# A gated mix of windowed attention and a state-space convolution: channel order within a chunk, the transposition of x, and the loading of the parameters

## The chip, the cores and the metric

The kernel runs on one core of a Trainium2 chip. The metric is device time in microseconds: the median of three runs is 471.79 us (470.23 to 472.16). The core has five engines with a queue of instructions each, worked off in order: PE (matrix products, with separate weight loads, PEld), ACT and DVE (elementwise work; both can read the matmul results in PSUM), POOL and SP (here they mainly issue DMAs). ACT, SP and POOL each issue DMAs on a queue of their own.

## The reference

x has 2048 positions and 640 channels. The result is `g * a + (1 - g) * b`, position by position.

```python
g = _sigmoid((x * gate_w).sum(-1, keepdims=True))
# a: 32 heads of 20, each query sees 8 keys at distances 0, 2, ..., 14
qkv = (x @ wqkv).reshape(B, S, 3, H, Dh)
logits = jnp.einsum("bhsd,bhswd->bhsw", q, kg) * Dh ** -0.5
a = einsum("bhsw,bhswd->bhsd", softmax(logits), vg).reshape(B, S, D) @ wo
# b: one kernel of length 2048 per channel out of 192 complex modes, then a causal convolution by FFT
P = jnp.exp((dt * A)[:, :, None] * l[None, None, :])
K = jnp.einsum("dn,dnl,dn->dl", Cc, P, dt * Bc).real
y = irfft(rfft(pad(x)) * rfft(pad(K)))[:L] + x * Dskip
```

A = A_re + i A_im, Bc and Cc likewise, are 640 x 192 each; dt = exp(log_dt) is one number for each channel.

## The kernel before

**Parameters.** `SSMParams.loads` brings the six 640 x 192 tensors into SBUF as 128 partitions x 5 x 192, channel 5p + k in partition p at k: one DMA each, three on SP's queue and three on ACT's, followed on SP by four quarters of x in its natural layout (`xn`, L67) and on POOL by five slices of wqkv (L68). `part` turns them into phases and magnitudes, split into 12 bf16 pieces per mode, in two parts: k = 0 alone (part A, all at once) and k = 1 to 4 (part B, whose steps are spread over the first ticks of what follows). Each piece is written to a DRAM buffer `Sprm` by SP (L372, L374) and comes back, chunk by chunk, as `L` (`load_L`, L476, SP).

**Chunks.** `KGen.chunk` works on 64 channels at a time, ten chunks (c = 0 to 9). For a chunk, PE forms arguments in PSUM (L498), ACT takes their sine (L509, 12 instructions) or exponential (L516, 6), DVE multiplies, and PE sums over the modes (L550). Every such ACT instruction is followed by `drain`, which advances a tick; 18 ticks make a chunk. At a tick `tick_hook` inserts work of other parts into the instruction streams: a step of part B, steps of the projections (`late`), and steps of the attention (`core`, 0.56 steps per tick from tick 25 on).

**Attention.** `window` transposes the first half of x on PE, with the identity, ahead of the chunks: 40 matmuls (L85) into PSUM and five ACT copies (L86) to `xT`. `late` has 70 steps: 15 projections of the first quarter of positions, ten transposes of the second half (L105, L106), 45 projections. A projection is five accumulating matmuls of 128x512 (L140) and an ACT copy (L142); one or two of them make a store on POOL's queue (L144) to q, k or v in DRAM, from where `core` loads them (L182 to L184, POOL). The gate is computed from all of xT at tick 31.

**FFT.** After the chunks, x and the kernels go through a first DFT stage (L651, evacuated by `copy_on`, L691 on ACT and L693 on DVE, in turn), a second (L739, L742), a product, and an inverse: 20 groups of 16 matmuls 64x128 (L768) into PSUM tiles `cp`, each copied to `C` by `copy_on` (ACT or DVE), then the last stage (L782) and the output. `C` holds 160 channels contiguously for each of 128 rows; `chan(c, q)` says at which of the 80 places of a half the channel q of chunk c lies. With 5p + k as above, neighbouring channels of a chunk lie 5 apart.

What `copy_on` writes for group cb, four channels l:

```python
def chan(c, q):
    return 40 * (c % 2) + 5 * q + c // 2
x0 = chan(cb // 2, 4 * (cb % 2))
dst = C.rearrange("p x (c q) -> p x c q", c=2)[:, :, :, x0:x0 + 16:5]
copy_on(nc, cb, dst, cp[:].rearrange("p c l x -> p x c l"))
```

Of the kernel before, what the change touches and what calls it, by code (L numbers as in the profile page):

```python
# [10 lines left out]
ACT = mybir.ActivationFunctionType  # L11
ALU = mybir.AluOpType
AX = mybir.AxisListType
F32 = mybir.dt.float32
BF16 = mybir.dt.bfloat16
# [6 lines left out]
D = 640  # L22
# [5 lines left out]
NKT = 5  # L28
SC = 512
# [18 lines left out]
class Attn:  # L48
# [10 lines left out]
    def loads(self, bufA, xn, cst):  # L59
# [3 lines left out]
        self.xn = xn  # L63
        xr = self.x.rearrange("(i p) d -> p i d", p=128)
        wr = self.wqkv.rearrange("(k p) c -> p k c", p=128)
        self.gw = cst.tile([128, NKT], BF16, name="gw_sb")
        xl = [lambda sc=sc: nc.sync.dma_start(xn[:, 4 * sc:4 * sc + 4], xr[:, 4 * sc:4 * sc + 4]) for sc in range(4)]  # L67
# [3 lines left out]
    def window(self, cst, pa):  # L71

        nc = self.nc
        xn, xT, ident = self.xn, self.xT, self.ident

        def zeros():
            zz = cst.tile([128, 5, HALO], BF16, name="zz")
            nc.vector.memset(zz[:], 0.0)
            nc.gpsimd.dma_start(self.kS[:, :, 0:HALO], zz[:])
            nc.gpsimd.dma_start(self.vS[:, :, 0:HALO], zz[:])  # L80

        def transpose(hf, kt):
            tx = pa.tile([128, 2, 512], F32, name="ar")
            for i in range(8):
                nc.tensor.matmul(tx[:, i // 4, (i % 4) * 128:(i % 4) * 128 + 128], xn[:, 8 * hf + i, kt * 128:(kt + 1) * 128], ident[:], start=True, stop=True)  # L85
            nc.scalar.activation(xT[:, kt, 1024 * hf:1024 * hf + 1024], tx[:].rearrange("p a b -> p (a b)"), ACT.Identity)  # L86
        zeros()
        for kt in range(NKT):
            transpose(0, kt)
# [9 lines left out]

    def transposes(self, sc):  # L100
        nc = self.nc
        for kt in range(NKT):
            tx = self.slot()
            for i in range(4):
                nc.tensor.matmul(tx[:, i * 128:i * 128 + 128], self.xn[:, 4 * sc + i, kt * 128:(kt + 1) * 128], self.ident[:], start=True, stop=True)  # L105
            nc.scalar.activation(self.xT[:, kt, SC * sc:SC * sc + SC], tx, ACT.Identity)  # L106
            yield
# [21 lines left out]
    def proj(self, wk, sc):  # L129
# [3 lines left out]
        for which, dstS, off in ((0, self.qS, 0), (1, self.kS, HALO), (2, self.vS, HALO)):  # L133
            for e in range(5):
# [8 lines left out]
                if e % 2 == n - 1:  # L143
                    nc.gpsimd.dma_start(dstS[:, e + 1 - n:e + 1, off + c0:off + c0 + SC], t[:, 0:n])  # L144
                yield

    def late(self, wk):
        yield from self.proj(wk, 0)
        for sc in range(2, NSC):
            yield from self.transposes(sc)  # L150
        for sc in range(1, NSC):
            yield from self.proj(wk, sc)
# [12 lines left out]
    def load_wo(self):  # L165
        self.nc.gpsimd.dma_start(self.wo_sb[:], self.wo.rearrange("(p e) c -> p e c", e=5))
# [99 lines left out]
def chan(c, q):  # L266

    return 40 * (c % 2) + 5 * q + c // 2
# [39 lines left out]
class SSMParams:  # L308
# [5 lines left out]
    def loads(self, ctx, tc, A_re, A_im, B_re, B_im, C_re, C_im, log_dt, gate_w, ident, gw_sb, pa, xl, wl):  # L314
# [3 lines left out]
        self.t = t = {}  # L318

        def load(eng, nm, ap):  # L320
            t[nm] = pin.tile([128, 5, NST], BF16, name=nm)
            eng.dma_start(t[nm][:], ap.rearrange("(p k) n -> p k n", k=5))
        ldt = pin.tile([128, 5], BF16, name="ldt")
        lg5 = pin.tile([5, 128], BF16, name="lg5")
        nc.sync.dma_start(ldt[:], log_dt.rearrange("(p k) -> p k", k=5))
        load(nc.sync, "cre", C_re); load(nc.scalar, "bre", B_re)
        load(nc.sync, "cim", C_im); load(nc.scalar, "bim", B_im)
        load(nc.sync, "aim", A_im); load(nc.scalar, "are", A_re)
        nc.sync.dma_start(lg5[:], gate_w.rearrange("(k p) -> k p", p=128))
        xl[0](); xl[1]()  # L330
        for w_ in wl:
            w_()
        xl[2](); xl[3]()
# [4 lines left out]
        nc.scalar.activation(self.dtb[:], ldt[:], ACT.Exp)  # L338
        nc.vector.tensor_tensor(self.dt2[:], self.dtb[:], self.dtb[:], ALU.mult)
        lt = pa.tile([128, 2, 512], F32, name="ar")  # L340
        nc.tensor.matmul(lt[:, 0, 0:5], lg5[:], ident[0:5, 0:5], start=True, stop=True)
        nc.scalar.activation(gw_sb[:], lt[:, 0, 0:5], ACT.Identity)

    def part(self, pool, tc, k0, nk, hold):
# [3 lines left out]
        cre, cim, bre, bim, are, aim = (self.t[n][:, k0:k0 + nk] for n in ("cre", "cim", "bre", "bim", "are", "aim"))  # L348
# [92 lines left out]
class KGen:  # L441
    def __init__(self, cst, tc, prm):
# [3 lines left out]
        for i in range(2):  # L446
            L = cst.tile([128, 2, 2, 2 * NST], BF16, name=f"L{i}")
            nc.gpsimd.memset(L[:], 0.0)
            for g2 in range(2):
                nc.gpsimd.memset(L[64 * g2:64 * g2 + 2], 1.0)  # L450
            self.Lb.append(L)
# [8 lines left out]
    def consts(self):  # L460
        nc = self.nc
        nc.gpsimd.dma_start(self.R[:], nc.inline_tensor(_arg_consts(), name="c_rarg").ap())
        nc.gpsimd.dma_start(self.S12[:], nc.inline_tensor(_shift_consts(), name="c_s12").ap())
# [192 lines left out]
def fft_prefetch(ctx, tc, x, omS):  # L656
# [8 lines left out]
    P["xn"] = pre.tile([128, 16, D], BF16, name="xn", tag="uga")  # L665
# [31 lines left out]
def fft_conv(ctx, tc, P, kx, gaS, out2d):  # L697
# [61 lines left out]
    with tc.tile_pool(name="ff_ps3", bufs=4, space=PSUM) as ps3, tc.tile_pool(name="ff_psr2", bufs=1, side="right") as psr2, \  # L759
# [3 lines left out]
        for cb in range(20):  # L763
# [7 lines left out]
            dst = C.rearrange("p x (c q) -> p x c q", c=2)[:, :, :, x0:x0 + 16:5]  # L771
# [32 lines left out]
def gated_mix_kernel(ctx, tc, A_x, A_wqkv, A_wo, B_A_re, B_A_im, B_B_re, B_B_im, B_C_re, B_C_im, B_log_dt, B_Dskip, gate_w, out):  # L804
# [24 lines left out]
    xl, wl = at.loads(P["bufA"], P["xn"], acst)  # L829
# [9 lines left out]
    at.window(acst, pa)  # L839
    for st_ in range(7):  # L840
        psteps.pop(0)()
    Dk = keep.tile([128, 2, NCH, CQ], BF16, name="Dk")
    Dn = keep.tile([128, 160], BF16, name="Dn")
    nc.gpsimd.memset(Dn[:], 0.0)
# [131 lines left out]
```

## Time and profile before

| | us |
|---|---|
| median of the runs (lowest, highest) | 471.79 (470.23, 472.16) |
| profiled execution | 468.3 |
| its span, from first to last instruction | 466.5 |
| PE / DVE / ACT / POOL busy | 354.7 / 335.1 / 351.5 / 85.4 |
| first exponential of chunk 0 (ACT) | 36.5 |
| first copy from cp | 411.95 |
| first matmul of the last stage | 444.47 |
| mean granted clock of PE | 0.90 of full |

The profile is of one execution. Busy time is per engine; what set the time at a place is read from the chain of waits and from the timeline. In a row of the costliest groups stand the source line, engine, operation, output and input, the count, and then: busy time in us, mean ns of one, idle time of the engine before them and what ended it. The chain of work that ended last is 35% PE, 26% ACT, 18% DVE, 9% issue, 8% DMA. The granted clock is 1.0 or 0.5 in stretches; it is 0.5 over most of the time from 412 to 447 us.

### The profile page before, as it was taken

To read this page: it belongs to the slowest core of one execution; us is meant where nothing else is said; L and a number is where in the kernel's file an instruction comes from. 1 tells how busy PE (TensorE), PEld (TensorE's weight loads), DVE (VectorE), ACT (ScalarE), POOL (GpSimd) and SP (SyncE) were. 2 spreads that over 40 slices of the span, in tenths; PEclk is the share of its full clock that TensorE was granted. 3 is DMA by queue.
4 is the path that set the end of the run, shared out by engine and by line. 5 is a ranking of instruction groups with operands and counts; after the bars stand their busy time and mean duration, and the time that the engine had idled before them with its cause. 6 is when DMAs were issued, how large, how long until landed. Compare 5 with 4: busy or idle time off the path is not lost.

```text
span 466.5 us, 11435 instructions
## 1 busy us (share of the span) xinstructions
PE 354.7 (76%) x4886; PEld 204.0 (44%) x4886; DVE 335.1 (72%) x409; ACT 351.5 (75%) x498; POOL 85.4 (18%) x123
## 2 busy tenths in 40 slices
PE   1557499988986989996899988778685799666480
PEld 0312155443532454543444444444484555455380
DVE  5996746778688454869846697832585598989972
ACT  3879998868749686575875699958474799869972
POOL 8611124221512213011112300000000010000033
PEclk9979599889997999999999999997988999955586
DMA  8944347552845454146643433020189722130046
GB/s 287 358 129 112 107 145 200 138 134 66 227 104 128 115 180 126 42 140 212 179 142 101 138 98 103 4 85 0 47 318 201 131 69 68 45 137 1 1 86 141
DMA packets 55725, 58.81 MB, mean 126 GB/s; under 512 B 39530, under 2 KB 47610, under 8 KB 55418
## 3 DMA queue, kind: packets, MB, share of 16 engines
q1 hardware_dynamic: 46954, 29.26, 23.6%
q0 software_dynamic: 7984, 26.74, 19.9%
q10 hardware_dynamic: 736, 2.08, 1.2%
q8 instruction: 38, 0.62, 0.6%
q14 instruction: 13, 0.11, 0.1%
HBM read 38.29 MB, written 19.77 MB: 124 GB/s over the span
## 4 chain that ended last, share of the span: by engine, by line
PE 35%; ACT 26%; DVE 18%; issue 9%; DMA 8%; POOL 2%; ACTq 0%; SPq 0%; POOLq 0%; DVEq 0%
PE tb L140 10%; DVE bufA L693 8%; PE tb L223 5%; PE fp L739 4%; PE ar L498 3%; ACT exq L516 3%; ACT prj L142 3%; PE tb L233 3%; ACT trg L509 3%; ACT sp_u L742 2%; ACT sp_k L742 2%; PE lg L190 2%; PE lg L140 2%; PE bp L651 2%; DMA kc<-kS 2%
## 5 line engine op out<-in xcount | busy, mean ns | idle before, releaser
L509 ACT ACTIVATE trg<-ar 128x608 bf16<-128x608 int16 x120 | 79.5, 695 | 3.6 <-PE ar L498 3.4
L498 PE MATMUL ar<-Rarg,L 64*128 64x216 bf16 (+1 forms) x480 | 63.7, 291 | 18.7 <-ACT trg L509 11.4
L140 PE MATMUL tb<-bufA 128*128 128x512 bf16 x260 | 72.3, 405 | 5.8 <-ACT prj L142 4.1
L188 DVE TENSOR_TENSOR prod<-qc,kc 128x2048 bf16<-128x2048 bf16 x40 | 47.9, 1218 | 22.0 <-PE lg L190 9.1
L220 DVE TENSOR_TENSOR pv<-vc,asb 128x4096 bf16<-128x4096 bf16 (+1 forms) x24 | 46.0, 1931 | 17.1 <-DMA asb<-aS 11.7
L516 ACT ACTIVATE exq<-ar 128x864 bf16<-128x864 f32 x60 | 51.2, 897 | 2.3 <-issue 2.0
L140 PEld LDWEIGHTS <-bufA 128*128 128x128 bf16 x300 | 33.9, 122 | 41.6 <-issue 21.3
L142 ACT ACTIVATE prj<-tb 128x512 bf16<-128x512 f32 x52 | 31.3, 601 | 26.8 <-PE tb L140 16.2
L498 PEld LDWEIGHTS <-L 64*128 64x128 bf16 x480 | 23.0, 95 | 53.7 <-issue 49.0
L539 DVE TENSOR_TENSOR pt<-trg,exq 128x1024 bf16<-128x1024 bf16 x30 | 20.7, 689 | 34.8 <-ACT trg L509 19.4
L550 PE MATMUL kps<-qq,pt 128*32 128x22 bf16 (+1 forms) x2560 | 41.5, 177 | 4.5 <-DVE qq L541 3.1
L223 PE MATMUL tb<-pv,ident 128*128 128x512 bf16 (+1 forms) x192 | 41.3, 352 | 4.0 <-DVE pv L220 2.3
L550 PEld LDWEIGHTS <-pt 128*32 128x32 bf16 (+1 forms) x2560 | 27.0, 91 | 36.7 <-issue 27.0
L691 ACT ACTIVATE bufA<-cp 128x1024 bf16<-128x1024 f32 x10 | 31.7, 3514 | 5.4 <-PE cp L768 5.4
L693 DVE CAST bufA<-cp 128x1024 bf16<-128x1024 f32 x10 | 31.7, 3414 | 2.0 <-PE cp L768 2.0
L739 PEld LDWEIGHTS <-PHI 128*128 128x128 bf16 x256 | 24.8, 97 | 18.5 <-issue 8.3
L768 PE MATMUL cp<-GAB,Y 64*128 64x128 bf16 x320 | 19.3, 307 | 16.5 <-DVE bufA L693 11.3
L233 PE MATMUL tb<-wo_sb,oT 128*128 128x320 bf16 x160 | 27.6, 304 | 3.2 <-ACT ga L234 2.1
L541 DVE TENSOR_TENSOR qq<-trg,exq 128x1408 bf16<-128x1408 bf16 x30 | 26.5, 884 | 0.0
L223 PEld LDWEIGHTS <-ident 128*128 128x128 bf16 x192 | 18.1, 98 | 19.0 <-issue 6.4
L224 ACT ACTIVATE oT<-tb 128x512 bf16<-128x512 f32 (+1 forms) x24 | 12.8, 532 | 16.6 <-PE tb L223 16.6
L768 PEld LDWEIGHTS <-Y 64*128 64x128 bf16 x320 | 17.0, 141 | 18.8 <-issue 13.1
(190 smaller groups left out, 618.1 us busy)
## 6 DMA issues: line engine op xcount, KB each, us to landing
asb<-aS SPq DMA_DIRECT2D x8, 512.0 KB
PSI<-c_psi SPq DMA_DIRECT2D x8, 512.0 KB
PHI<-c_phi POOLq DMA_DIRECT2D x8, 384.0 KB, 3.6
L<-Sprm SPq DMA_DIRECT2D x80, 36.0 KB
kc<-kS POOLq DMA_DIRECT2D x8, 337.5 KB, 5.1
vc<-vS POOLq DMA_DIRECT2D x8, 337.5 KB, 4.7
xn<-in_A_x_dram SPq DMA_DIRECT2D x4, 640.0 KB
qc<-qS POOLq DMA_DIRECT2D x8, 320.0 KB, 4.4
```

Source lines behind the costliest of these rows:

```text
L140: nc.tensor.matmul(ppf, self.wq[:, kt, which * D + e:(which + 1) * D:5], self.xT[:, kt, c0:c0 + SC], start=(kt == 0), stop=(kt == NKT - 1))
L142: nc.scalar.activation(t[:, e % 2, :], ppf, ACT.Identity)
L188: nc.vector.tensor_tensor(prod[:], qc[:, e, :].unsqueeze(1).to_broadcast([128, W, C]), win(kc[:, e, :], 0, W, DIL, C), ALU.mult)
L220: nc.vector.tensor_tensor(pv[:, :, 0:n, :], for_e, asb[:].unsqueeze(2).to_broadcast([128, W, n, C]), ALU.mult)
L223: nc.tensor.matmul(op[:, 0:n, :], ident[:], pv[:, w, 0:n, :], start=(w == 0), stop=(w == W - 1))
L233: nc.tensor.matmul(apf[:, :320], oT[:, e, i * 128:(i + 1) * 128], wo_sb[:, e, hf * 320:(hf + 1) * 320], start=(e == 0), stop=(e == 4))
L498: nc.tensor.matmul(ar[:, g2, a0:a0 + ncol], L[rows, gp, sub, m0:m0 + 128], R[rows, c0:c0 + ncol], start=True, stop=True, tile_position=(64 ...
L509: ins = nc.scalar.activation(dst[:, 2 * gp:2 * gp + 2, sub, :], ar[:].bitcast(I16)[:, :, 0:2 * SW:2], ACT.Sin, scale=SCL)
L516: self.last = nc.scalar.activation(dst[:, 2 * gp:2 * gp + 2].rearrange("p g s n -> p g (s n)"), ar[:, :, 0:2 * EW], ACT.Exp)
L550: nc.tensor.matmul(kps[32 * g:32 * g + 32, c2, NM * ql:NM * ql + NM], pt[rows, 8 * g + ql, v, :], qq[rows, 8 * g + ql, v, :], start=(key n ...
L693: nc.vector.tensor_copy(o, i)
L739: nc.tensor.matmul(fp[:, fl, 0:320].rearrange("p (c x) -> p c x", x=32), PHI[:, fl, kind, :], B[:, :, 2 * f1 + ri].rearrange("p c q g -> p ...
```

## The change

Four things change together. (1) Parameters are loaded so that channel 80a + 16k + b lies in partition 16a + b at k: one DMA of 128 rows of 384 bytes for each tensor and k, 30 instead of 6, part A's first. A chunk's eight channels are then neighbours, `chan(c, q) = 8c + q`, and the copies to `C` write four neighbouring channels. log_dt is loaded as rows beside gate_w and turned on PE with it. (2) x's quarters are loaded by transposing DMAs straight into `xT`; `xn` and all PE transposes go. (3) wqkv is issued ahead of the memsets of `L` on POOL; `Dk` is loaded in place, without the two POOL copies; `wo` is issued after the store of the projections that precedes it. (4) `late` has 60 steps, ten of them issued ahead of chunk 0, the rest at other ticks.

```diff
@@ loads
-        xl = [lambda sc=sc: nc.sync.dma_start(xn[:, 4 * sc:4 * sc + 4], xr[:, 4 * sc:4 * sc + 4]) for sc in range(4)]
+        xl = [lambda sc=sc: nc.sync.dma_start(self.xT[:, :, SC * sc:SC * sc + SC], self.x[SC * sc:SC * sc + SC], transpose=True) for sc in range(4)]
@@ window
-        def transpose(hf, kt):
...
-        for kt in range(NKT):
-            transpose(0, kt)
-    def transposes(self, sc):
...
     def late(self, wk):
-        yield from self.proj(wk, 0)
-        for sc in range(2, NSC):
-            yield from self.transposes(sc)
-        for sc in range(1, NSC):
+        for sc in range(NSC):
             yield from self.proj(wk, sc)
@@ load_wo
-        self.nc.gpsimd.dma_start(self.wo_sb[:], self.wo.rearrange("(p e) c -> p e c", e=5))
+        after(self.tc, self.nc.gpsimd.dma_start(self.wo_sb[:], self.wo.rearrange("(p e) c -> p e c", e=5)), self.stored)
@@ chan
-    return 40 * (c % 2) + 5 * q + c // 2
+    return 8 * c + q
@@ SSMParams.loads
-        load(nc.sync, "cre", C_re); load(nc.scalar, "bre", B_re)
-        load(nc.sync, "cim", C_im); load(nc.scalar, "bim", B_im)
-        load(nc.sync, "aim", A_im); load(nc.scalar, "are", A_re)
-        nc.sync.dma_start(lg5[:], gate_w.rearrange("(k p) -> k p", p=128))
-        xl[0](); xl[1]()
+        def load(eng, nm, k0, nk):
+            t[nm, k0] = pin.tile([128, nk, NST], BF16, name=f"{nm}{k0}")
+            for k in range(k0, k0 + nk):
+                eng.dma_start(t[nm, k0][:, k - k0], src[nm].rearrange("(a k b) n -> k a b n", k=5, b=16)[k])
...
+        for nm in ("cre", "cim", "aim"):
+            load(nc.sync, nm, 0, 1)
+        for nm in ("bre", "bim", "are"):
+            load(nc.scalar, nm, 0, 1)
+        nc.sync.dma_start(lg10[5:10], gate_w.rearrange("(k p) -> k p", p=128))
+        for nm in ("bre", "bim"):
+            load(nc.scalar, nm, 1, 4)
+        load(nc.sync, "cre", 1, 4)
+        load(nc.sync, "cim", 1, 4)
+        xl[0]()
         for w_ in wl:
             w_()
-        xl[2](); xl[3]()
+        load(nc.sync, "aim", 1, 4)
+        load(nc.gpsimd, "are", 1, 4)
+        for x_ in xl[1:]:
+            x_()
@@ fft_conv
-            dst = C.rearrange("p x (c q) -> p x c q", c=2)[:, :, :, x0:x0 + 16:5]
+            dst = C.rearrange("p x (c q) -> p x c q", c=2)[:, :, :, x0:x0 + 4]
@@ gated_mix_kernel
-        NLATE = 70
+        NLATE = 60
-                    state["core"] = at.core(c2, g_sb, ps, lambda sc: late_to((15, 40, 55, 70)[sc]))
+                    state["core"] = at.core(c2, g_sb, ps, lambda sc: late_to(15 * (sc + 1)))
-            late_to(n if n < 30 else 30 + int((n - 30) * 0.4))
+            late_to(10 + n if n < 20 else 30 + int((n - 20) * 0.3))
         kg.hook = tick_hook
+        late_to(10)
```

## The prediction

> **What bounds the kernel now.** I read the page first: which engine is busy when, and what the costliest groups are.
>
> ```profile
> span 466.5 us, 11435 instructions
> PE 354.7 (76%) x4886; PEld 204.0 (44%) x4886; DVE 335.1 (72%) x409; ACT 351.5 (75%) x498; POOL 85.4 (18%) x123
> ...
> PEclk9979599889997999999999999997988999955586
> ...
> L691 ACT ACTIVATE bufA<-cp 128x1024 bf16<-128x1024 f32 x10 | 31.7, 3514 | 5.4 <-PE cp L768 5.4
> L693 DVE CAST bufA<-cp 128x1024 bf16<-128x1024 f32 x10 | 31.7, 3414 | 2.0 <-PE cp L768 2.0
> ```
>
> No engine is full for the whole span, so each stage has its own limit. The last tenth shows a low granted clock and two groups of copies at about 3.5 us each. The timeline shows that stage:
>
> ```profile
> 411.95 31.71 ACT L691 ACTIVATE bufA<-cp 128x1024 bf16<-128x1024 f32 x10 [5.36 <-PE cp L768]
> 412.74 31.67 DVE L693 CAST bufA<-cp 128x1024 bf16<-128x1024 f32 x10 [1.98 <-PE cp L768]
> ...
> 416.37 1.89 PE L768 MATMUL cp<-GAB,Y 64*128 64x128 bf16 x32 [0.93 <-DVE bufA L693]
> ...
> 444.47 6.33 PEld L782 LDWEIGHTS <-PSI 128*128 128x128 bf16 x73 [3.69 <-DVE bufA L693]
> ```
>
> ACT and DVE copy without a pause; PE works 1.89 of every 3.38 us and waits. From the first copy to the first inverse matmul (411.95 to 444.47) are 32.5 us, all set by these 20 copies. The groups by shape show copies of the same size by the same two lines that are three times faster:
>
> ```profile
> L693 DVE CAST Bu<-bp 128x1024 bf16<-128x1024 f32 x10 | 11.5, 1216 | 1.4 <-PE bp L651 1.4
> L691 ACT ACTIVATE Bu<-bp 128x1024 bf16<-128x1024 f32 x10 | 9.7, 1022 | 2.7 <-PE bp L651 2.2 <-DMA kc<-Kx 0.5
> ```
>
> At the start I read the chain of waits and the busy times by stretch:
>
> ```profile
> 13.18 0.91 ACT bufA L86
> ...
> 18.45 0.92 ACT bufA L86
> 19.36 0.04 issue
> 19.41 1.01 PE ar L85 x8
> ...
> 21.27 0.87 PE ar L85 x8
> 22.14 0.02 issue
> 22.16 1.02 ACT bufA L86
> ...
> 36.52 0.89 ACT exq L516
> ```
>
> ```profile
> 68.00:72.00 4.00, 3.87 (x111) 2.79 (x111) 2.09 (x3) 4.00 (x9) 2.78 (x4) 1.00 0.50 135
> ```
>
> The TensorE transposes of x and their copies lie on the chain that leads to the first chunk. Later (the second number is PE, the fourth pair ACT) ACT is full at 68 to 72 us, where the other ten L106 copies run between the sines.
>
> **The change, part by part.** The sums go against the profiled execution, 468.3 us (span 466.5 and 1.8 around it); the median shown, 471.8, is 3.5 above, and I add that at the end.
>
> *The 20 copies behind L768.* Their destination step goes from 10 bytes (5 channels of 2 bytes) to runs of four channels, 8 bytes. The PSUM side keeps its steps. Bu copies also read PSUM in steps and write runs of 16 channels, at 1.02 (ACT) and 1.22 us (DVE), both engines at once. Unknown is whether 8 bytes are a long enough run: bounds are 1.0 to 1.2 us as for Bu, and 3.4 to 3.5 as now. I take the Bu end, since the destination then fills neighbouring bytes as there. With 0.06 us between copies, a DVE copy each 1.28 us gives 10 x 1.28 = 12.8 us, plus 1.2 for the first, 14.0: a gain of 18.5. But PE needs 1.89 / 2 = 0.945 us for each bank pair at the clock 0.5 that it has here, 20 x 0.945 + 1.2 = 20.1 us if it stays cold: a gain of 12.4. In the next stage the clock is back at 1.00 once PE is over 90% busy, so between them: **-16** (bounds 0 and -18.5).
>
> [...]
>
> *The first half of x, L85 and L86.* 40 transposes and 5 copies of 1.0 us go. On the chain above they hold 0.91 + 0.92 + 1.01 + 0.87 + 1.02 = 4.7 us. In their place ten projections, instead of four, are issued ahead of the first chunk: six more, 5 matmuls of 0.24 us and a copy of 0.6 us each, so 6 x 1.2 = 7.3 us of PE, which waits for those copies anyway from 24 to 30 us, and 3.6 us of ACT. Between 4.7 off and 7.3 on, partly side by side: **+1** (bounds -4 and +7).
>
> *The second half, L105 and L106.* Up to tick 30 the old schedule takes 20 projections and ten transposes, the new one 23 projections beyond the ten: ACT 20 x 0.60 + 10 x 0.74 = 19.4 against 13.8 us. The full stretch of ACT is where they sat (sine and copy together every 1.03 us, sine alone about 0.55), so most of it counts: **-5** (bounds 0 and -8).
>
> *Ticks 30 to 130.* Forty projections were left, now 27: 13 fewer, 13 x 5 x 0.244 = 15.9 us of PE, 7.8 of ACT. They move to the start, where PE is half idle. PE is 16 to 18 of 20 us busy here, but the chain changes hands between PE, ACT, DVE and POOL's stores and loads of q, k, v. POOL's queue is in order: a store that waits for its copy (59.1 us in 12 waits for kS) holds the qc and kc loads behind it, and scores wait for kc. Projections of the second quarter now end by tick 20, ahead of those loads. I count under half: **-7** (bounds 0 and -16).
>
> *The loads.* Six parameter loads become 30 of 48 KB: SP issues 15 where it issued 3, ACT 11 where it issued 3, POOL 4 more. At 0.45 us each ACT's first table load and dtb move from 3.9 to about 7.6 us; DVE first needs dtb at 8.1 (tau), and ACT's next work is at 7.5 us now, so this is just covered; without that cover it would be 3.6 us. Packets go from 1920 to 384 bytes. Between 30 and 40 us such packets cost 0.35 x 10 x 16 / 2320 = 24 ns; 3840 of them on 16 engines are 5.8 us instead of 4.5 at the rate of the first 12 us.
>
> ```profile
> q1 hardware_dynamic: 2131, 2.67, 67.6%
> ```
> ```profile
> q1 hardware_dynamic: 2320, 0.79, 35.0%
> ```
>
> The first line (0 to 12 us) gives 49 ns per KB, so x's 2.62 MB took 8 us of all engines. What a transposing load takes, no row shows. Low end: the same 8 us, hidden as now. High end: SP spends 0.47 us on issuing an L load of 36 KB; at that rate four quarters are 71 x 0.47 = 33 us. All four quarters now stand ahead of the Sprm writes (L374) on SP's queue; the last of these is issued at 28.6 us, and L's loads and the first argument matmul (33.0) wait for it. SP reaches the first quarter after 13 issues, about 6 us; with aim's four (1.6) and 33 us the queue is free at 41: +12. I take the low end with a little contention from wqkv, which POOL now issues at 2.5 instead of 10.7 us, since the same bytes go between the same places: **+2** (bounds 0 and +12). L's memsets (8.4 us on POOL) move behind wqkv and are done by about 16, well before L is loaded; their cover ends at 28 us. The first projections need x's first quarter by about 24 us, when ACT can take their result. Two POOL copies of Dk (1.2 us) go for nothing: POOL is 18% busy.
>
> [...]
>
> *Sum*: -16 + 1 - 5 - 7 + 2 = -25: 468.3 - 25 = 443.3, and 3.5 on top for the median: **447**, own range 437 to 458.
>
> **The rivals.** *The copies stay slow* (8-byte runs still cost one access for each element, or the PSUM side is the limit: the view of this tile has 2.4 us for the shortest copy and 3.7 for the median, so two at once share something). Then -16 falls to between 0 and -8, 455 to 463, and up to 468 if the middle gives nothing too. Against it: the Bu copies. *SP's queue is held by the transposing loads.* Place: L374's writes behind them. Price: 7.6 + T against 28.6 us, T for the four quarters. The gains apart from the loads are 27, so beyond T = 48 us (55 GB/s) the kernel is slower; at T = 70 it is 471.8 - 27 + 49 = 494. For it: the order on SP, and no row that bounds such a load. Against it: the plain loads move 333 GB/s over the first 20 us. *The middle gains all of it and the copies reach 14 us*: 471.8 - 18.5 + 1 - 8 - 16 + 2 = 432. *The change of order does nothing*, gains and a late first chunk cancelling at T near 48: within 0.5%.
>
> **How the numbers follow.** Forecast 0.52; copies stay slow 0.20; more gained than 437: 0.07; cancelled, 0.05; SP held, slower, 0.16. The predicted time is the forecast's, 447. Of the extremes I leave out the slow case and a little below, so 433 to 473. Faster by over 0.5% (2.4 us, about what a measurement can tell from no change): 0.52 + 0.20 + 0.07 = 0.79; within: 0.05; slower: 0.16.
>
> **What would show it.** Right: the copies behind the 64x128 matmuls near 1.1 us, and 14 to 20 us from the first of them to the inverse matmuls; a first exponential near 37 us; no full ACT stretch with L106; the Sprm writes issued by 30 us. Wrong: copies above 2 us; SP issuing the last Sprm write of the first part after 35 us; chunks that still take as long in the middle. A transposing load above 12 us a quarter would turn the sign.

## The result and the profile after

| | before | after |
|---|---|---|
| median of the runs, us (lowest, highest) | 471.01 (469.77, 472.16) | 452.13 (449.92, 456.55) |
| ratio, with its 95% interval | 1 | 0.961 (0.953 to 0.970) |
| profiled execution / its span, us | 468.3 / 466.5 | 449.92 / 448.1 |
| first exponential of chunk 0 | 36.5 | 52.0 |
| last exponential or sine of chunk 9 | 329.3 | 333.3 |
| first copy from cp | 411.95 | 416.30 |
| first matmul of the last stage | 444.47 | 429.13 |

The kernel became faster by 18.9 us. The times of the stages in the table are starts. The table splits the 18.4 us of the two profiled executions into stages, by subtraction: the first exponential comes 15.5 us later; from there to the last function of the ten chunks are 281.3 us where there were 292.8 (-11.5); the middle stage up to the first copy is even (83.0 against 82.7); the stage of the copies takes 12.8 us for 32.5 (-19.7); and from the first inverse matmul to the end are 19.0 us for 22.0 (-3.0).

The page of the kernel after, its first rows and the granted clock in 40 slices:

```profile
span 448.1 us, 11301 instructions
PE 336.5 (75%) x4806; PEld 188.4 (42%) x4806; DVE 312.9 (70%) x409; ACT 324.8 (72%) x485; POOL 87.0 (19%) x125
...
PEclk9995996988889999989998999989996979998897
```

The low clock at the end is gone (the last five slices have 9, 8, 8, 9, 7 where 5, 5, 5, 8, 6 stood), and PE waits less there. The timeline of the copies behind the cp matmuls (start, duration of the group, engine, line, then the instruction and its count):

```profile
415.17 12.32 PE L749 MATMUL cp<-GAB,Y 64*128 64x128 bf16 x316 [1.85 <-DVE Y L738]
416.30 1.02 ACT L672 ACTIVATE bufA<-cp 128x1024 bf16<-128x1024 f32 x1 [5.36 <-PE cp L749]
...
418.80 10.28 DVE L674 CAST bufA<-cp 128x1024 bf16<-128x1024 f32 x9 [0.48 <-PE cp L749]
419.41 8.46 ACT L672 ACTIVATE bufA<-cp 128x1024 bf16<-128x1024 f32 x8 [0.44 <-PE cp L749]
...
429.13 5.15 PE L763 MATMUL yp<-bufA,PSI 128*128 128x160 bf16 x72 [1.64 <-DVE bufA L674]
```

A copy takes 1.02 us on ACT and 10.28 / 9 = 1.14 us of pace on DVE, where they took 3.5 and 3.4 us. The timelines of SyncE's and ScalarE's queues at the start of the same kernel show the loss:

```profile
3.80 7.27 SPq L297 DMA_DIRECT2D cre<-in_B_C_re_dram  x4
14.33 4.50 SPq L297 DMA_DIRECT2D cim<-in_B_C_im_dram  x4
18.88 4.59 SPq L65 DMA_TRANSPOSE bufA<-in_A_x_dram  x1
23.52 2.52 SPq L297 DMA_DIRECT2D aim<-in_B_A_im_dram  x4
26.09 9.39 SPq L65 DMA_TRANSPOSE bufA<-in_A_x_dram  x3
35.59 1.49 SPq L356 DMA_DIRECT2D Sprm<-pc  x3
...
43.80 7.57 SPq L458 DMA_DIRECT2D L<-Sprm  x16
...
4.16 11.49 ACTq L297 DMA_DIRECT2D bre<-in_B_B_re_dram  x4
15.73 2.67 ACTq L297 DMA_DIRECT2D bim<-in_B_B_im_dram  x4
18.44 1.28 ACT L322 ACT_TABLE_LOAD   x1 [18.44 <-DMA bim<-in_B_B_im_dram]
...
26.02 0.36 ACT L352 ACTIVATE pc<-tau 128x192 bf16<-128x192 f32 x1 [4.45 <-DVE tau L345]
```

Four issues of bre hold ScalarE's queue for 11.49 us, where an issue took 0.47 before. The table load behind them starts at 18.44 instead of 2.65, the first finished piece of the parameters (pc from tau) at 26.02 instead of 11.34, and L's first load at 43.80 instead of 30.39. On SyncE the three later transposing loads end at 35.48, and the first stores of Sprm go out right behind them. The later ones wait for ScalarE: between 37.08 and 42.80 SyncE waits 3.8 us for two pieces of part B, whose stores stand ahead of L's loads in its queue, and 0.6 us for one of part A, whose last store is issued at 41.45. So at the end it was ScalarE's pieces, and not the transposing loads, that L waited for. The ten projections ahead of chunk 0 then add to it on PE:

```profile
39.08 2.29 PE L116 MATMUL lg<-bufA 128*128 128x512 bf16 x5 [8.51 <-ACT prj L118]
...
49.98 0.36 PE L480 MATMUL ar<-Rarg,L 64*128 64x216 bf16 x4
```

The first argument matmul comes 6.2 us after the first load of L; in the runs without ten projections ahead it comes 2.6 (before), 3.1 (experiment 7) and 2.8 us (experiment 8) after it.

The view of waits of SyncE's queue over the first 36 us shows that issues of parameter loads wait for other loads to land, also for one that ScalarE issued:

```profile
SPq L297 <- DMA cre<-in_B_C_re_dram: 3.8, 2, 3.2
SPq L297 <- DMA bim<-in_B_B_im_dram: 1.5, 1, 1.5
```

(us in total, times, longest.) The same view of the kernel before has two such waits at a distance of eight places: of the DMAs of SyncE and ScalarE in the order of their issue, the ninth (of gate_w) waits 0.2 us for the first (ident), and the eleventh (of x) 1.2 us for the third (bre). That fits theory C of experiment 4, an issue that waits for the load eight places before it, but no view says what makes an issue wait, and the distance was not varied, so this cause is not shown. That kernel issued 13 such DMAs ahead of its first store of Sprm; this one issues 33. What the traces do show is that an issue that waits holds its whole queue: the table load at 18.44 stands behind bim's issues.

### The profile page after: what moved, and what is told of

The parts are those of the page before. It is cut to its first block, busy times and chain, and to the rows that moved or that the text cites. A ratio compares the mean times of both kernels' runs of the same rounds, so it can differ in the third digit from the quotient of the medians.

```text
span 448.1 us, 11301 instructions
## 1 busy us (share of the span) xinstructions
PE 336.5 (75%) x4806; PEld 188.4 (42%) x4806; DVE 312.9 (70%) x409; ACT 324.8 (72%) x485; POOL 87.0 (19%) x125
## 4 chain that ended last, share of the span: by engine, by line
PE 36%; ACT 19%; DVE 13%; DMA 10%; issue 7%; POOL 1%; SPq 1%; ACTq 0%; POOLq 0%; DVEq 0%
PE tb L116 7%; PE tb L196 6%; PE fp L720 4%; PE tb L206 4%; PE ar L480 4%; DVE bufA L674 3%; DMA kc<-kS 3%; PE bp L633 3%; ACT exq L498 3%; ACT sp_u L723 2%; PE lg L163 2%; DVE prod L161 2%; ACT sp_k L723 2%; ACT prj L118 2%; ACT ga L207 2%
## 5 line engine op out<-in xcount | busy, mean ns | idle before, releaser
L491 ACT ACTIVATE trg<-ar 128x608 bf16<-128x608 int16 x120 | 76.9, 681 | 5.4 <-PE ar L480 4.8
L480 PE MATMUL ar<-Rarg,L 64*128 64x216 bf16 (+1 forms) x480 | 59.4, 285 | 16.3 <-ACT trg L491 9.8
L116 PE MATMUL tb<-bufA 128*128 128x512 bf16 x220 | 59.9, 403 | 2.3 <-ACT prj L118 1.4
L193 DVE TENSOR_TENSOR pv<-vc,asb 128x4096 bf16<-128x4096 bf16 (+1 forms) x24 | 45.7, 1928 | 19.7 <-DMA asb<-aS 17.2
L196 PE MATMUL tb<-pv,ident 128*128 128x512 bf16 (+1 forms) x192 | 44.6, 372 | 3.6 <-DVE pv L193 1.8
L116 PE MATMUL lg<-bufA 128*128 128x512 bf16 x80 | 23.4, 429 | 26.7 <-DMA bufA<-in_A_x_dram 16.0
L532 PE MATMUL kps<-qq,pt 128*32 128x22 bf16 (+1 forms) x2560 | 37.5, 175 | 6.1 <-DVE E L884 2.3
L118 ACT ACTIVATE prj<-tb 128x512 bf16<-128x512 f32 x44 | 26.5, 601 | 21.0 <-PE tb L116 13.4
L521 DVE TENSOR_TENSOR pt<-trg,exq 128x1024 bf16<-128x1024 bf16 x30 | 20.6, 686 | 20.2 <-ACT exq L498 10.4
L163 PE MATMUL lg<-prod,ind 128*32 128x512 bf16 x160 | 22.7, 417 | 11.5 <-DVE prod L161 8.0
L196 PEld LDWEIGHTS <-ident 128*128 128x128 bf16 x192 | 18.7, 102 | 22.6 <-issue 11.2
L651 POOL DMA_DIRECT2D PHI<-c_phi x8 | 4.4, 548 | 112.6 <-PE fp L720 109.4
L207 ACT ACTIVATE ga<-tb,g_sb 128x320 bf16<-128x320 f32 x32 | 17.1, 534 | 9.1 <-PE tb L206 8.1
```

What stands on the lines that cost most here:

```text
L116: nc.tensor.matmul(ppf, self.wq[:, kt, which * D + e:(which + 1) * D:5], self.xT[:, kt, c0:c0 + SC], start=(kt == 0), stop=(kt == NKT - 1))
L118: nc.scalar.activation(t[:, e % 2, :], ppf, ACT.Identity)
L163: nc.tensor.matmul(lg[32 * b:32 * b + 32], ind[:], prod[:, :, 64 * b:64 * b + 64], start=(e == 0), stop=(e == 4), skip_group_check=True, t ...
L193: nc.vector.tensor_tensor(pv[:, :, 0:n, :], for_e, asb[:].unsqueeze(2).to_broadcast([128, W, n, C]), ALU.mult)
L196: nc.tensor.matmul(op[:, 0:n, :], ident[:], pv[:, w, 0:n, :], start=(w == 0), stop=(w == W - 1))
L480: nc.tensor.matmul(ar[:, g2, a0:a0 + ncol], L[rows, gp, sub, m0:m0 + 128], R[rows, c0:c0 + ncol], start=True, stop=True, tile_position=(64 ...
```

## The experiments

All ratios are to the kernel before, with a 95% interval. Milestones are of one profiled execution each; those of all experiments stand in the table behind the last one.

**1. The copies alone.** The kernel before with only the destination of the 20 copies made contiguous. The output's channels come in another order, with the same work otherwise.

```diff
-            x0 = chan(cb // 2, 4 * (cb % 2))
-            dst = C.rearrange("p x (c q) -> p x c q", c=2)[:, :, :, x0:x0 + 16:5]
+            x0 = 4 * cb
+            dst = C.rearrange("p x (c q) -> p x c q", c=2)[:, :, :, x0:x0 + 4]
```

> The kernel before, with only the destination of the 20 copies to C changed to runs of four neighbouring channels; the channels in C, and so in the output, stand in another order than the reference's. If the tail's gain in the changed kernel (22.7 us from the first of these copies to the end) comes from the step of the copies alone, the copies take 1.0 to 1.2 us, the stage 12 to 14 us, the rest after it 19 us, and the time is 446 to 450 us. If part of it needs something else of the change (the earlier release of buffers, the other schedule), the time is 452 us or more.

One run: 451.24 us, against a median of 471.15 for the kernel before beside it. Its copies in the timeline:

```profile
417.34 9.72 ACT L691 ACTIVATE bufA<-cp 128x1024 bf16<-128x1024 f32 x9 [0.62 <-PE cp L768]
418.00 10.28 DVE L693 CAST bufA<-cp 128x1024 bf16<-128x1024 f32 x9 [0.28 <-PE cp L768]
...
428.33 5.15 PE L782 MATMUL yp<-bufA,PSI 128*128 128x160 bf16 x72 [1.64 <-DVE bufA L693]
```

First copy to end: 33.8 us, where there were 54.6: 12.6 for 32.5 in the stage of the copies, and 21.2 for 22.0 behind it, where 19 had been expected. So in this one run the order of the channels in C alone gives about as much as the whole change, and everything else in the change adds up to about nothing. The 2 us by which the last stage of the kernel after is shorter still (19.0) do not come from the copies.

**2. Sixteen groups instead of eight in the parameter loads.** A part's rows are in 16 groups of 8 instead of 8 groups of 16; the channels follow in runs of 8.

```diff
-    return 8 * c + q
+    return 40 * (c % 2) + 8 * (c // 2) + q
...
-                eng.dma_start(t[nm, k0][:, k - k0], src[nm].rearrange("(a k b) n -> k a b n", k=5, b=16)[k])
+                eng.dma_start(t[nm, k0][:, k - k0], src[nm].rearrange("(a k b) n -> k a b n", k=5, b=8)[k])
```

> The changed kernel with another order of channels: channel 40a + 8k + b in partition 8a + b, so that each parameter load steps over 16 groups of rows instead of 8 (Dk permuted on POOL again). A chunk's eight channels stay neighbours. Theory A, the loads run on as many DMA engines as there are groups, 8 of 16: the loads land twice as fast, the first exponential comes at 44 us or before instead of 52, and the time is 441 to 447 us. Theories B (wqkv ahead) and C (few DMAs in flight): first exponential within 3 us of 52, time 449 to 456.

449.15 us (445.11 to 451.60), ratio 0.953 (0.945 to 0.960). The four issues of bre take 6.08 us for 11.49, those of cre 5.08 for 7.27, those of cim 3.22 for 4.50; the table load starts at 16.50, the first exponential at 47.5. The interval overlaps that of the kernel after, so the total does not separate the two; the queues do. Neither theory's sign is met: the first exponential lies between the 44 of the one and the 49 to 55 of the others.

**3. wqkv later.** wqkv is loaded behind the memsets of L (13.1 us) instead of at 2.5 us.

```diff
-        for w_ in wl:
-            w_()
...
+    for L in kg.Lb:
+        nc.gpsimd.memset(L[:], 0.0)
...
+    for w_ in wl:
+        w_()
```

> The changed kernel with POOL's five wqkv loads issued after the memsets of L (near 13 us) as in the kernel before, instead of at 2.5 us. Theory B, wqkv takes the DMA engines from the small parameter loads: these land in 2 to 3 us each, ACT's table load comes at 11 us or before instead of 18.4, the first exponential at 45 us or before, time 441 to 448. Theory A: ACT's table load within 2 us of 18.4, time 450 to 457.

444.73 us (442.18 to 446.10), ratio 0.943 (0.936 to 0.951). The table load starts at 10.80 and the four issues of bre take 3.77 us; the parts of are, issued by POOL, land 3.0 us after their issue (median) where they took 8.6 in the kernel after. The first exponential comes at 46.0, 1 us beyond the 45 expected, and the later transposing loads now meet wqkv:

```profile
11.27 2.99 SPq L65 DMA_TRANSPOSE bufA<-in_A_x_dram  x1
17.00 17.29 SPq L65 DMA_TRANSPOSE bufA<-in_A_x_dram  x3
34.41 1.47 SPq L354 DMA_DIRECT2D Sprm<-pc  x3
```

The view of the DMAs from 9 to 17 us of this run, in 40 slices of 0.2 us, shows the parameter loads by themselves until the first transposing load (11.27 us) and wqkv (13.1 us) begin (tenths of 16 engines, and GB/s):

```profile
DMA  5544544444433354522688799899999999399299
GB/s 136 131 108 98 144 127 121 115 133 121 113 104 94 88 138 127 119 56 58 168 202 174 118 216 197 140 234 292 291 288 287 292 289 616 128 384 538 115 499 538
```

Up to 11.2 us the engines are half busy and move 90 to 145 GB/s, although nothing else is loading. In the kernel before, the whole tensors and the first of x came with 289 GB/s over the first 12 us. The half-busy row and the shorter issues of experiment 2 (6.08 us for 11.49) agree with theory A of that experiment, eight of 16 engines for eight groups, but no view here names the engines of one transfer, so the theory is not shown. The pace of the issues is a rival that was not separated from it: in experiment 5, SyncE alone issues 16 parts without a wait, at 0.62 us each (2.49 / 4), and from 9 to 13 us 80 GB/s are moved, which is 48 KB in 0.62 us. Two queues at that pace would move 160 GB/s, an estimate from this number.

**4. ScalarE without the later loads.** The later parts of B_re and B_im are issued by SyncE; ScalarE keeps the first parts.

```diff
-        for nm in ("bre", "bim"):
-            load(nc.scalar, nm, 1, 4)
-        load(nc.sync, "cre", 1, 4)
-        load(nc.sync, "cim", 1, 4)
+        for nm in ("cre", "bre", "bim", "cim"):
+            load(nc.sync, nm, 1, 4)
```

> The changed kernel with the eight later loads of B_re and B_im issued by SP instead of ACT. Theory C, an issue waits until the load eight before it has landed, and what stands behind it in the queue waits too: ACT is free at 4.2 us, its first activation comes when log_dt has landed (10.5 us) instead of at 19.7, the first part's chain and the first exponential 6 to 9 us earlier, time 443 to 448. If ACT's late start is not what delays the first chunk (theories A, B: the data themselves come late), the first exponential stays within 3 us of 52 and the time at 449 to 456.

444.07 us (442.68 to 451.97), ratio 0.942 (0.935 to 0.948). From the timelines of the two queues:

```profile
4.16 1.28 ACT L320 ACT_TABLE_LOAD   x1 [4.16 <-issue]
...
20.99 2.89 SPq L65 DMA_TRANSPOSE bufA<-in_A_x_dram  x1
26.50 8.41 SPq L65 DMA_TRANSPOSE bufA<-in_A_x_dram  x3
35.03 1.96 SPq L354 DMA_DIRECT2D Sprm<-pc  x4
```

The table load is 14.3 us earlier, yet the first exponential only 4.5 (47.5), where 6 to 9 had been expected. SyncE's queue now holds the stores of Sprm until 35.03, but they do not come last. The chain of waits of this run goes from SyncE's issues of parts and the landing of cim (23.24) over steps of VectorE and ScalarE to the projections on PE:

```profile
33.30 0.49 ACT prj L118
33.79 0.04 issue
33.83 2.29 PE lg L116 x5
...
45.40 0.29 PE ar L478 x4
```

So behind ScalarE's queue stood other waits, and the last of them are the projections that the change itself puts ahead of chunk 0.

**5. Both: wqkv later and ScalarE free.** The edits of experiments 3 and 4 together.

```diff
-        for nm in ("bre", "bim"):
-            load(nc.scalar, nm, 1, 4)
...
+        for nm in ("cre", "bre", "bim", "cim"):
+            load(nc.sync, nm, 1, 4)
...
-        for w_ in wl:
-            w_()
...
+    for w_ in wl:
+        w_()
```

> Both edits together: POOL issues wqkv after the memsets of L, and SP instead of ACT issues the later loads of B_re and B_im. If the two remove separate delays, the first exponential comes at 40 to 43 us (46.0 and 47.5 with one of them) and the time falls to 438 to 442 us. If a third thing now ends the wait, SP's queue, where three transposing loads stand ahead of the Sprm writes (issued from 34.4 and 35.0 us on with one edit each, right after the last transposing load), the first exponential stays at 45 us or later and the time at 443 to 447.

456.14 us; the four runs spread from 447.18 to 458.18 and the profiled one is the longest, so there is no ratio. SyncE's timeline in that longest one:

```profile
14.34 14.63 SPq L65 DMA_TRANSPOSE bufA<-in_A_x_dram  x1
34.29 12.00 SPq L65 DMA_TRANSPOSE bufA<-in_A_x_dram  x3
```

Two edits that each save 7 to 8 us gave nothing together in three of the four runs; what was different in the run of 447.18 no trace shows. In the profiled one, the first transposing load falls into wqkv's transfer and holds the queue for 14.63 us; in experiments 3 and 4 a first one took 2.99 and 2.89. The parts of aim stand behind it, and VectorE waits 11.86 us for them, until 40.33.

**6. Three quarters of x behind L of chunk 0.** Experiment 5, with the last three transposing loads after the loads of L for chunk 0.

```diff
-        for x_ in xl[1:]:
-            x_()
...
-    Ls = {0: kg.load_L(0), 1: kg.load_L(1)}
+    Ls = {0: kg.load_L(0)}
+    for x_ in xl[1:]:
+        after(tc, x_(), kg.lastL)
+    Ls[1] = kg.load_L(1)
```

> The same, and the last three transposing loads of x are issued behind the loads of L for chunk 0, so that no Sprm write of the first part waits behind them. If SP's queue is what holds the first chunk, the Sprm writes start by 25 us, the first exponential comes at 36 to 41 us, and the time is 433 to 440 us. If not, or if the projections of the second quarter now wait for x, it is within 3 us of the run with both edits, or above it.

452.71 us (449.38 to 456.59), ratio 0.962 (0.955 to 0.968). L's loads start at 37.25, the first exponential at 44.7, but the three loads then hold SyncE from 41.02 to 53.67, ahead of the loads of L for chunk 1. The queue is held later instead of earlier. The time misses the 433 to 440 us expected, and so does the first exponential (36 to 41). The first store of Sprm is issued at 26.91, but the first transposing load holds the queue for 9.65 us ahead of aim's parts, VectorE waits for these until 28.92, and behind that stand the projections.

**7. The pace of the projections as before.** No projections ahead of chunk 0, then 20 by tick 30 and 0.4 for each tick after.

```diff
-            late_to(10 + n if n < 20 else 30 + int((n - 20) * 0.3))
+            late_to(int(n * 2 / 3) if n < 30 else 20 + int((n - 30) * 0.4))
...
-        late_to(10)
```

> The changed kernel with the projections at the old pace: none ahead of chunk 0, 20 by tick 30, then 0.4 a tick. If the shorter stretch of the ten chunks (281 us from first exponential to last table function, against 293 before) comes from moving projections to the start, it grows by 6 to 16 us; the first exponential comes 2 to 5 us earlier for want of the ten; time 453 to 464. If the stretch is shorter because the transposes and their copies are gone, it stays within 3 us of 281 and the time is 447 to 452.

457.08 us (455.46 to 458.60), ratio 0.973 (0.968 to 0.978). The first exponential comes 3.9 us sooner (48.1), but the ten chunks take 291.7 us, as before. In the kernel after, the first two chunks are longer than before (64.9 us for 56.1) and the other eight shorter (216.4 for 236.7); here they are 54.6 and 237.1. So the gain in the chunks comes from the projections that are moved to the start, and hardly any from the transposes that are gone (291.7 against 292.8 us). Of the 10.4 us gained in the chunks, 3.9 are paid at the start.

**8. x by TensorE, parameters part by part.** The kernel before with the channels in natural order, the parameters loaded part by part and wqkv issued early, both as in the kernel after; x is loaded plainly and transposed on TensorE as before, at the old pace.

```diff
-    return 40 * (c % 2) + 5 * q + c // 2
+    return 8 * c + q
...
-        load(nc.sync, "cre", C_re); load(nc.scalar, "bre", B_re)
...
+                eng.dma_start(t[nm, k0][:, k - k0], src[nm].rearrange("(a k b) n -> k a b n", k=5, b=16)[k])
...
-            dst = C.rearrange("p x (c q) -> p x c q", c=2)[:, :, :, x0:x0 + 16:5]
+            dst = C.rearrange("p x (c q) -> p x c q", c=2)[:, :, :, x0:x0 + 4]
```

> The kernel before with the natural order and the parameters loaded part by part as in the changed kernel (wqkv ahead of the memsets too), but x in its natural layout, transposed on PE, and the old schedule of 70 steps. If the small loads behind eight in flight and behind wqkv delay the start, the first exponential comes at 46 us or later with plain loads of x as well, and the time is the tail's gain less that delay: 456 to 463 us. If the transposing loads of x delay it, the first exponential comes at 37 to 42 us and the time is 447 to 453.

463.62 us (460.79 to 471.92), ratio 0.985 (0.978 to 0.993). From the timeline of ScalarE's queue:

```profile
4.14 11.76 ACTq L324 DMA_DIRECT2D bre<-in_B_B_re_dram  x4
...
18.68 1.28 ACT L349 ACT_TABLE_LOAD   x1 [18.68 <-DMA bim<-in_B_B_im_dram]
```

No load transposes here, and the first exponential is late all the same: 50.0, 13.5 us after that of the kernel before. The part-by-part loads, with wqkv's early issue beside them, make the late start; the transposing loads and the ten projections ahead add 2.0 to it in the kernel after.

**9 to 11. Whole loads.** In 9 the kernel before writes C contiguously, and the last stage brings the channels into the reference's order when it reads yp:

```diff
-                    for l in range(4):
-                        nc.scalar.activation(th[:, l], yp[:, l // 2, 160 * (l % 2):160 * (l % 2) + 160], ACT.Identity, scale=om32[:, t0 + l:t0 + l + 1])
+                for l in range(4):
+                    o = th[:, l].rearrange("p (c s q j) -> p c s q j", c=2, s=2, q=8)
+                    i = yp[:, l // 2, 160 * (l % 2):160 * (l % 2) + 160].rearrange("p (c j s q) -> p c s q j", c=2, j=5, s=2)
+                    om = om32[:, t0 + l:t0 + l + 1]
...
+                        nc.vector.tensor_scalar(o, i, om, None, ALU.mult)
...
+                        nc.scalar.activation(o, i, ACT.Identity, scale=om)
```

> The kernel before with one stage written otherwise: the twenty copies of the cp tile write their four channels side by side, in the order of the chunks, and the channels are put into the reference's order when the last stage reads yp (on ScalarE with the four instructions it had, on VectorE with four scalings in place of one product). Loads, projections and ticks stay as before. If the distance of 10 bytes between the channels was the whole of the slow stage, it is gone as in the run with the copies alone: the first copy to the end takes 33 to 35 us, the total 447 to 453 us. If reading yp in a permuted order costs what writing C in steps of 10 bytes did, the last stage grows from 22 us to 35 or more and the total is 463 us or more.

Experiment 10 is the kernel after with that last stage and the six whole parameter loads of the kernel before, wqkv behind the memsets of L, and two quarters of x behind L; 11 is the same with wqkv early.

```diff
-                eng.dma_start(t[nm, k0][:, k - k0], src[nm].rearrange("(a k b) n -> k a b n", k=5, b=16)[k])
...
+            eng.dma_start(t[nm][:], ap.rearrange("(p k) n -> p k n", k=5))
...
+        xl[0](); xl[1]()
...
+    for x_ in xl[2:]:
+        after(tc, x_(), kg.lastL)
```

> The changed kernel's projections, ticks and transposing loads, with the parameters loaded as before in six whole tensors (so ScalarE's and SyncE's queues issue 2 and about 7 loads instead of 11 and 22), channels put into order in the last stage, wqkv behind the memsets of L, and the last two quarters of x behind L of chunks 0 and 1. Theory, that the late start is the part-by-part loads holding the two queues and little else: ScalarE's first exponential moves from 52 us to 37 to 42 us, the ten chunks still take 280 to 284 us, and the total is 433 to 441 us. Rival, that transposing loads hold SyncE's queue whatever the parameter loads are: the stores of Sprm are issued after 33 us, the first exponential comes at 45 us or later, the total is 444 us or more.

> The kernel of e10_whole_loads with wqkv issued at once, at about 2.5 us, as in the changed kernel. If the transposing loads meet wqkv's packets and this is what makes them slow, the first of them is issued before wqkv is in and takes 8 us or more on SyncE's queue, and the total is 5 us or more above e10_whole_loads. If only the parameters' small packets count, the two kernels agree within 3 us.

Experiment 9: 452.37 us (450.49 to 453.55), ratio 0.963 (0.958 to 0.968); first copy to end 36.0 us, 1 above what was expected. Reading yp in the permuted order, with four instructions on VectorE in place of one, costs about 2 us (36.0 against 33.8 in experiment 1), far from what writing C in steps did.

Experiment 10: 442.44 us (441.78 to 444.86), ratio 0.943 (0.938 to 0.948), 1.4 us above the expected range. SyncE's queue:

```profile
3.05 7.88 SPq L65 DMA_TRANSPOSE bufA<-in_A_x_dram  x2
17.05 5.34 SPq L344 DMA_DIRECT2D Sprm<-pc  x3
...
38.82 6.56 SPq L65 DMA_TRANSPOSE bufA<-in_A_x_dram  x2
```

The start is nearly that of the kernel before (37.6 against 36.5) with ten projections ahead, and the chunks keep their 281.2 us: the theory holds for both. What is missing is at the end: 35.7 us from the first copy where the kernel after takes 31.8, and 86.4 instead of 83.0 in the middle stage, which lies between 80.7 and 86.4 in all runs and was not explained.

Experiment 11: 445.82 us (442.74 to 448.27), ratio 0.947 (0.940 to 0.954). The first two transposing loads hold SyncE for 14.94 us instead of 7.88, and the view gives 14.9 us from issue to landing instead of 7.2, so meeting wqkv does slow them, but the start loses only 2.2 us (39.8; with the parameters in parts, wqkv's early issue cost 6) and the intervals of 10 and 11 overlap. Whether the total pays for it stays open.

**12. The permutation by the matmul.** Experiment 10 with the last stage of the kernel before, and C read in the reference's order as the moving operand:

```diff
-                                         C[:, 64 * ro + t2, :],
+                                         C[:, 64 * ro + t2, :].rearrange("p (c j x) -> p c x j", c=2, j=5),
```

> The kernel of e10_whole_loads, whose last stage is again that of the kernel before, and whose matmuls of yp read C as their moving operand in the reference's order of channels (16 runs of 5 elements 32 bytes apart, for each half) instead. If a moving operand is read in any order at one price, a matmul of the last stage keeps its duration (2.94 us for the first 40), the first copy of the cp tile to the end takes 32 to 34 us instead of 35.7, and the total is 437 to 441 us. If TensorE pays for the steps as the copies did, by a factor of two or more, the last stage's 128 matmuls take 10 us more and the total is 448 us or more. The start is that of e10_whole_loads: the first exponential at 36 to 39 us.

464.25 us (462.93 to 468.98), ratio 0.989 (0.983 to 0.994); the start is as expected (37.9). The rival holds, and by more than it said:

```profile
419.49 36.96 PE L747 MATMUL yp<-bufA,PSI 128*128 128x160 bf16 x128 [1.64 <-DVE bufA L658]
```
```profile
440.00:464.00 24.00, 16.45 (x58) 6.87 (x56) 6.26 (x12) 6.23 (x20) 5.77 (x10) 0.50 0.30 69
```

The 128 matmuls take 36.96 us, 289 ns each; in experiment 10 the first 40 took 2.94 us, 74 ns each. The second line (the busy times by stretch, 440 to 464 us) shows that PE, at the granted clock of 0.50 there, sets the pace: it is busy without a pause up to the last of these matmuls, at 456.45, and ACT and DVE for a quarter of the 24 us.

The milestones of the profiled executions, in us. "Rest" is the span less the end of the chunks:

| | first exponential | ten chunks | end of the chunks | rest | span |
|---|---|---|---|---|---|
| before | 36.5 | 292.8 | 329.3 | 137.2 | 466.5 |
| after | 52.0 | 281.3 | 333.3 | 114.8 | 448.1 |
| 1 copies alone | 36.7 | 293.5 | 330.2 | 119.3 | 449.5 |
| 2 sixteen groups | 47.5 | 282.1 | 329.6 | 113.7 | 443.3 |
| 3 wqkv later | 46.0 | 281.2 | 327.2 | 115.4 | 442.6 |
| 4 ScalarE free | 47.5 | 280.4 | 327.9 | 114.8 | 442.7 |
| 5 both | 56.2 | 281.9 | 338.1 | 118.1 | 456.2 |
| 6 x behind L | 44.7 | 286.8 | 331.5 | 115.8 | 447.3 |
| 7 old pace | 48.1 | 291.7 | 339.8 | 117.0 | 456.8 |
| 8 x by TensorE | 50.0 | 292.1 | 342.1 | 117.3 | 459.4 |
| 9 permuted last | 36.8 | 293.9 | 330.7 | 121.1 | 451.8 |
| 10 whole loads | 37.6 | 281.2 | 318.8 | 122.1 | 440.9 |
| 11 the same, wqkv early | 39.8 | 284.8 | 324.6 | 121.9 | 446.5 |
| 12 permuted by the matmul | 37.9 | 284.9 | 322.8 | 141.6 | 464.4 |

Experiments 3, 4 and 10 beat both kernels; of these 3 and 4 are the smallest edits of the kernel after, and their intervals and that of 10 overlap.

## Why the prediction was right in sum, point by point

The time, 452.1 us, lies in the range and 5 us above the 447 predicted; the profiled executions differ by 18.4 us where the sum of the terms was 25. Two terms were mis-sized, in opposite directions: -22.7 + 2.0 - 11.5 + 13.5, and 0.3 in the middle stage, make the -18.4. That the time still lies in the range is partly luck: the 6.7 us too little for the copies and the 11.5 too little for the loads offset each other.

- *The 20 copies, -16.* Measured -22.7 from the first copy to the end, beyond the bound of -18.5; experiment 1 gives -20.8 of it to the copies alone. The cause is the one named, an order of neighbouring bytes. The mistake was to go half way towards a cold PE. With the short copies PE is granted 0.90 over their stage (0.91 in experiment 1, from 412 to 430 us) where it had 0.50, and the copies set the pace, as for Bu. So the stage itself gave 19.7. The last stage gave 3.0 more, which the prediction did not count. Of this the copies explain 0.8: in experiment 1 PE's 128 matmuls there take 9.28 us, as in the kernel after (9.29), for 10.59 before, and yet the stage takes 21.2. The chain of waits there runs over a store of the output, which VectorE waits for (3.3 us in the kernel before, 2.8 in the kernel after); why the stage is shorter in the kernel after stays open. No run varied the step, so the runs show the gain but not why a step of 10 bytes is slow.
- *The first half of x, +1.* Experiment 8 against the kernel after gives +2.0, transposing loads and ten projections together. Within the bounds.
- *L105 and L106, -5, and ticks 30 to 130, -7.* Together -12, measured -11.5, but not shared out so. Experiments 7 and 8 differ in the transposes alone of what runs in the chunks, 291.7 against 292.1 us, so the -5 is worth about nothing over the ten chunks. The first two are 2.8 us shorter without the transposes (54.6 against 57.4 us), where the prediction saw ACT full; the others give it back. The projections moved to the start give about 10 there, and cost 3.9 at the start (experiment 7).
- *The loads, +2.* This is the step that failed. Experiment 8 gives +13.5 for the loads of the parameters in parts together with wqkv's early issue, beyond the bound of +12, which had been worked out for something else, the transposing loads. The prediction counted issues at 0.45 us and found ScalarE's table load at 7.6 us, "just covered". An issue of a part took 0.59 us at least, and most of the time was not the issues but their waits: ScalarE's eight later ones held its queue from 4.16 to 18.4. (The cover was thinner too: in the kernel before VectorE reads dtb at 6.91, for dt, and not first at 8.1.) The bytes were sized at 24 ns a packet on 16 engines, 5.8 us for all 30 parts, while they moved at 90 to 145 GB/s on half-busy engines (experiment 3), which for 30 parts of 48 KB is some 13 us at 115 GB/s; beside wqkv, VectorE waits for the last of bim until 23.99. "A little contention from wqkv" was priced at next to nothing; moving it away brought the first exponential 6 us forward.
- *Which rival came near.* "SP's queue is held" was placed right in part: the first Sprm writes did go out right behind the transposing loads, at 35.59, and the last of part A at 41.45, where "after 35 us" had been set as the sign. But the last ones waited for ScalarE's pieces and not for the transposing loads, and in the chains of waits of experiments 4 and 6 the projections ahead of chunk 0 come last. The rival put the cause on T, the time of the four quarters. T was 4.59 + 9.39 = 14 us of SyncE's queue, far below the 48 us at which the sign would have turned, and they started late, at 18.88 instead of 6, since the parameter loads stood before them. What a quarter takes from issue to landing, which no row of the kernel before showed, is 7.2 us in the view of experiment 10 (median) and 14.9 in that of experiment 11.
- *Dk, L's memsets.* Neither is on the chain; the memsets are done at 16.3 us.

## What to carry to other kernels

Before a load is cut into parts, ask what the issue of each part waits for and what else is loading then, not only what an issue costs: here issues that waited held their whole queue, and behind them stood the first function of the kernel (the table load, at 18.44 us for 2.65). Price each queue to its next consumer with all its issues, and expect another wait behind it when it is freed: here the steps of VectorE and ScalarE, and the projections issued ahead. Put a permutation where it is cheap (here the copy that wrote runs of 8 bytes, or the read of yp on ScalarE and VectorE), and never take a matmul's moving operand in another order without measuring it (289 against 74 ns here).

## What the runs showed of the hardware

- A step of 10 bytes in the destination made copies from 128x1024 f32 take 3.4 to 3.5 us with two engines at it; runs of 8 bytes took 1.02 us on ACT and 1.14 of pace on DVE, with the same steps on the PSUM side (kernel before and after; experiment 1 changes the destination alone).
- Reading PSUM in a permuted order with the same permuted writes into tt, and with four instructions on VectorE for one, cost 2 to 4 us from the first copy to the end (36.0 against 33.8 in experiments 9 and 1, 35.7 against 31.8 in experiment 10 and the kernel after). The same permutation as steps of 32 bytes in a matmul's moving operand cost a factor of 3.9 (289 against 74 ns for 128x160). How much of it is the clock's was not separated: it was 0.56 from 420 to 440 us and 0.50 from 440 to 464 in experiment 12, and 1.00 from 412 to 430 in experiment 10.
- A transposing load of 640 KB held SyncE's queue for 2.77 us in the kernel after (the second quarter, at 26.09) and for 14.63 us when it met wqkv's transfer (experiment 5). With wqkv's place as the only difference, two of them held it for 7.88 and for 14.94 us (experiments 10 and 11). Its packets are small: from 20 to 40 us, with four such loads, the kernel after moved 11,477 packets and 3.26 MB on that queue, 83.9% of 16 engines' time, 23 ns each (0.839 x 16 x 20 us / 11,477).
- PE's granted clock over the stage of the copies was 0.50 with the long copies, when PE was busy for 17.7 of 32.5 us, and 0.90 with the short ones of the kernel after (10.9 of 12.8 us). In the kernel before it was 1.00 from 448 to 452 us, with PE busy for 3.71 of 4 us. But in experiment 12 PE was busy for all of 36.96 us and was granted 0.56 from 420 to 440 us and 0.50 from 440 us on: a PE that counts as busy without a pause was not thereby at its full clock.
